# An adaptive layer norm block with a long convolution and a gated feed-forward: the inverse of an older step shares a PSUM bank with the spectrum of h, tables are built by half blocks, and loads change places

## The chip, the cores and the metric

The kernel runs on one core of a Trainium2 chip. Its engines are PE (TensorE: matmuls and transposes), DVE (VectorE), ACT (ScalarE), POOL (GpSimd) and SP (SyncE), which here issues all DMAs from one queue, in order. The metric is the device time in microseconds (us); lower is better. Before the change it is 1203.32 us, the median of three runs (1203.11 to 1203.95).

## The reference

One block of 2048 positions by 640 channels (D). A state space model gives each channel a kernel K as long as the sequence, and y is the causal convolution of h with K, written with Fourier transforms of twice the length. A gated feed-forward network of width 1728 follows. Cut to what matters:

```python
mod = (_silu(c) @ w_mod).reshape(c.shape[0], 6, 1, -1)
sa, ca, ga, sb, cb, gb = (mod[:, i] for i in range(6))
h = _layernorm(x) * (1 + ca) + sa
# _A_ref on h: 128 complex exponentials for each channel, summed
P = jnp.exp((A * dt[:, None])[:, :, None] * pos[None, None, :])
K = 2.0 * jnp.einsum("dn,dnl->dl", C, P).real
y = irfft(rfft(h, 2 * L) * rfft(K, 2 * L))[..., :L] + h * D_skip
x = x + ga * y
h = _layernorm(x) * (1 + cb) + sb
x = x + gb * ((_silu(h @ w1) * (h @ w3)) @ w2)
```

## The kernel before, in words

The channels are cut into five blocks of 128 (NB = 5). The work has these parts, which overlap.

- **h.** `h_stats` and `h_unit` normalise x (DVE, lines 257 and 260) and do the first stage of the transform of h as matmuls (line 267). The result goes to DRAM as h1.
- **Generation of K**, block by block (`gen_steps`). For each block, `param_part`, `param_exp` and `param_turn` make phases and decays, `param_exp` with eleven exponentials on ACT (line 340) into a tile E that has one buffer. `tables` builds small tables of powers by doubling: eight DVE instructions (lines 442 to 446) and twelve on POOL (line 449), for a block of 128 channels in one of two sets of tables. Then eight chunks of 16 channels each (`gen_chunk`) combine the tables: four POOL instructions (lines 480 and 486), three on ACT (sine, absolute value, cosine; lines 488 to 494), five on DVE (lines 498 to 502), and 32 small matmuls into kps (line 510; the profile counts 64 records). The next block's exponentials come with chunk 1, and its tables with chunks 2 to 6.
- **First stage of the transform of K** (`k_steps`): eight matmuls pk a block, copied to ko by ACT (line 575) and stored to DRAM as k1 (line 580). The last block does it in wide tiles (line 577).
- **The frequency stage** (`freq_steps`), also by block: 16 steps. A step has the spectrum of h (fh, line 602, evicted to fs by ACT, line 604), the spectrum of K (four matmuls fk, line 608), their product on DVE (fp, line 610), and, for the step two before (AH = 2), the first stage of the inverse (fz, two matmuls, line 619, evicted to zt, line 620). ht and kt are loaded for two steps at once (line 593); zt holds two steps, has two buffers, and is stored to DRAM as zd (line 622). fh, fk and fz each take a PSUM bank from the same three buffers (tag "f").
- **The last stage of the inverse** needs the factors wd, loads of zd (iz; for the last block of channels of the first rows izb; line 650), and x, to which its result is added. x lies in one tile x2 of 16 rows (j) per partition, and is loaded by `load_x2` (line 640). The first rows' inverse is done during the last frequency block (line 930).
- **The feed-forward** (`ffn`): second layer norm and transposes (`ln2`), then for four groups of 512 positions fourteen slices of the hidden width. `weights` loads a slice (w1 and w3 into wr, line 715 or 717; w2 into w2r, line 726 or 730) and splits it into a rounded part and a rest (lines 676 and 677, ACT and DVE). wr and w2r have two buffers each. The first slices are loaded before the feed-forward starts.

In the order of the program, block b's frequency stage lies beside the generation of block b + 1 and after. The order of the instructions on each engine is fixed when the program is built: a list scheduler takes the priorities that the kernel sets (`self.at`), and `order` adds an edge without a wait, which only says that one instruction is to stand behind another. On the chip each engine takes its instructions in that order, SP its DMA issues too.

Of the kernel before, what the change touches and what calls it, by code (L numbers as in the profile page):

```python
# [26 lines left out]
E4 = P // 4  # L27
EXPS = (1, 2, 4, 8, 16, 32)
# [69 lines left out]
class K:  # L98
# [318 lines left out]
    def table_sets(self):  # L417

        G = self.nc.gpsimd
        self.tabs = []  # L420
        for i in range(2):
            t = {nm: self.tbl.tile(sh, ty, name=f"{nm}{i}") for nm, sh, ty in (
                ("p1", [P, P, 2, 8], I32), ("p2", [P, P, 2, 4], I32),
                ("e1", [P, P, 2, 8], F32), ("e2", [P, P, 3, 4], F32))}
            G.memset(t["p2"][:, :, :, 0], 0)
            G.memset(t["e1"][:, :, :, 0], 1.0)
            G.memset(t["e2"][:, :, 2, 0], 1.0)
            self.tabs.append(t)
        self.step = self.tbl.tile([P, 4, 2, P], I32, name="step")

    def tables(self, b, part, parts, r=slice(0, P)):

        nc = self.nc
        V, G = nc.vector, nc.gpsimd
        t = self.tabs[b % 2]
        p1, p2, e1, e2 = (t[k] for k in ("p1", "p2", "e1", "e2"))
        E, st = self.E, self.step
        todo = []

        def steps():  # L440
            for a in range(2):
                V.tensor_scalar(p1[:, :, a, 0], self.pB[:, b, a], 0, None, op0=ALU.logical_shift_left)
            for k in range(1, 5):
                V.tensor_scalar(st[:, k - 1], self.pS[:, b], k, None, op0=ALU.logical_shift_left)
            for x, src in ((e2[:, :, 0, 0], self.mag[:, b]), (e2[:, :, 1, 0], E[:, 10])):
                V.tensor_copy(x, src)

        def double(tab, a, w, src, op):
            G.tensor_tensor(tab[:, r, a, w:2 * w], tab[:, r, a, 0:w], bc(src, len(src.shape), w), op=op)

        if r.start == 0:
            todo.append(steps)
        both = slice(0, 2)
        for tab, w, k in ((p2, 1, 3), (p2, 2, 4), (p1, 1, 0), (p1, 2, 1), (p1, 4, 2)):
            todo.append(lambda tab=tab, w=w, k=k: double(tab, both, w, (st[:, k - 1] if k else self.pS[:, b])[:, :, r].rearrange("p a t -> p t a"), ALU.add))
# [7 lines left out]
        return p1, p2, e1, e2  # L463


    def gen_chunk(self, d0, tabs, off, kps):
# [3 lines left out]
        p1, p2, e1, e2 = tabs  # L470
# [43 lines left out]
    def gen_steps(self, pc, ps):  # L514
# [7 lines left out]
        def chunk(c):  # L522
# [5 lines left out]
            self.gen_chunk(d0, self.cur, c * self.CD, st["kps"][:, (c % 2) * 256:(c % 2) * 256 + 256])  # L528
# [14 lines left out]
            if c == nch - 1:  # L543
                self.cur = self.nxt
# [41 lines left out]
    def freq_a(self, pc, fq, fpool, ps, bufs):  # L586
# [7 lines left out]
        return ht, kt, tl("zt")  # L594

    def freq_b(self, pc, fq, i, fpool, ps, bufs, held):

        nc = self.nc
        ht, kt, zt = held
        f = slice(2 * i, 2 * i + 2)  # L600
        ph = ps.tile([P, 512], F32, name=f"fh{pc}_{fq}{i}", tag="f", bufs=self.fb)[:, :2 * P].rearrange("p (f d) -> p f d", f=2)
        nc.tensor.matmul(ph, self.wh, ht[:, f, :], start=True, stop=True)  # L602
        hs = fpool.tile([P, 2, P], F32, name=f"fs{pc}_{fq}{i}", tag="fs", bufs=bufs["fs"])
        nc.scalar.activation(hs, ph, AF.Copy)
        pk = ps.tile([P, 2, 2, P], F32, name=f"fk{pc}_{fq}{i}", tag="f", bufs=self.fb)
        for g in range(2):
            for r in range(2):
                nc.tensor.matmul(pk[:, r, g], self.wb[:, 4 * fq + 2 * i + g, r, :], kt[:, 2 * i + g, :], start=True, stop=True)  # L608
        pp = fpool.tile([P, 2, 2, P], F32, name=f"fp{pc}_{fq}{i}", tag="fp", bufs=bufs["fp"])
        nc.vector.tensor_mul(pp, pk, bc(hs, 1, 2))  # L610
        return zt, pp

    def freq_c(self, pc, fq, i, ps, held):
        nc = self.nc
        o, n = pc * P, P
        zt, pp = held
        pz = ps.tile([P, 512], F32, name=f"fz{pc}_{fq}{i}", tag="f", bufs=self.fb)[:, :2 * P].rearrange("p (f d) -> p f d", f=2)
        for r in range(2):
            nc.tensor.matmul(pz, self.wz[:, r, :], pp[:, r], start=(r == 0), stop=(r == 1))  # L619
        nc.scalar.activation(zt[:, 2 * i:2 * i + 2], pz, AF.Copy)  # L620
        if i == 1:
            self.zlast = nc.sync.dma_start(self.zd[4 * fq:4 * fq + 4, :, :, o:o + n].rearrange("f r t d -> (r t) f d"), zt)

    def freq_steps(self, pc, fpool, ps, bufs, ahead=1):
        ha, hb = {}, {}

        def step(i):
            if i % 2 == 0 and i < 16:
                ha[i // 2] = self.freq_a(pc, i // 2, fpool, ps, bufs)
            if i < 16:  # L630
                hb[i] = self.freq_b(pc, i // 2, i % 2, fpool, ps, bufs, ha[i // 2])
            if i >= ahead:
                k = i - ahead
                self.freq_c(pc, k // 2, k % 2, ps, hb.pop(k))

        return [lambda i=i: step(i) for i in range(16 + ahead)]

    def load_x2(self, u, n, after):
        for q in range(4):
            self.order(self.nc.sync.dma_start(self.x2[q * 32:(q + 1) * 32, 2 * u:2 * (u + n)], self.xv[q, :, 2 * u:2 * (u + n), :]), after)  # L640
# [12 lines left out]
    def inverse(self, j0, nj, z, ps, tag, bufs, d0, d1, behind=None):  # L653
        nc = self.nc
        w = d1 - d0
        for j in range(nj):
            for o, n in ((0, w),) if w <= 512 else ((0, 320), (320, 320)):
# [7 lines left out]
                x2 = self.x2[:, j0 + j, d0 + o:d0 + o + n]  # L665
# [13 lines left out]
    def ln2(self, b, pool, ps, stats=None, tag="gu"):  # L679

        nc = self.nc
        xs = self.x2[:, b * 4:b * 4 + 4, :]
# [23 lines left out]
    def weights(self, b, m, wp):  # L706
# [3 lines left out]
        n = 2 if two else 1  # L710
        raw = wp.tile([P, 2, KT, P], F32, name=f"wr{b}_{m}", tag="wr", bufs=2)
        f0 = m * P
        for i, src in enumerate((self.w1, self.w3)):
            if two:
                nc.sync.dma_start(raw[:, i], src[:, f0:f0 + P].rearrange("(k p) f -> p k f", p=P))
            else:
                nc.sync.dma_start(raw[:, 0, :, i * 64:(i + 1) * 64], src[:, f0:].rearrange("(k p) f -> p k f", p=P))
# [7 lines left out]
        if two:  # L725
            nc.sync.dma_start(w2r, self.w2[m * P:(m + 1) * P, :])
            self.split(w2h, w2l, w2r, nc.vector)
        else:
            for i in range(2):
                nc.sync.dma_start(w2r[i * 64:(i + 1) * 64], self.w2[1664:1728, :])  # L730
# [75 lines left out]
    def output(self, b, acc, pool, ps):  # L806

        nc = self.nc
        for k in range(KT):
# [5 lines left out]
            xs = self.x2[:, b * 4:b * 4 + 4, k * P:(k + 1) * P]  # L815
            nc.vector.tensor_add(xs, pt.rearrange("p (j d) -> p j d", j=4), xs)
        for q in range(4):
            nc.sync.dma_start(self.ov[q, :, b * 4:b * 4 + 4, :], self.x2[q * 32:(q + 1) * 32, b * 4:b * 4 + 4, :])

    def run(self):  # L820
# [20 lines left out]
        e = open_("early", "right")  # L841
        self.gp = open_("gp")
# [16 lines left out]
        for r in (slice(0, 32), slice(32, P)):  # L859
            self.cur = self.tables(0, 0, 1, r)  # L860
# [26 lines left out]
        bufs = dict(ht=3, kt=3, fs=2, zt=2, fp=AH + 2)  # L887
        last = NB - 1
        stp = st0
        for pc in range(1, last + 1):  # L890
# [8 lines left out]
            for i, st in enumerate(self.freq_steps(pc - 1, fpool, psg, bufs, AH)):  # L899
# [8 lines left out]
        self.x2 = xp.tile([P, NJ, D], F32, name="x2")  # L908
        self.wd = ip.tile([P, NJ, 2, 64], F32, name="wd")
# [6 lines left out]
        for st in self.freq_steps(last, fpool, psg, bufs, AH):  # L916
# [8 lines left out]
        for u in range(2):  # L925
# [6 lines left out]
            x2 = self.x2[:, 2 * u:2 * u + 2, :cut]  # L932
            nc.vector.tensor_add(x2, py, x2)
            for j in (2 * u, 2 * u + 1):
                self.ln_part(stats[0], self.x2, j, 0, KT - 1)
# [9 lines left out]
        z = self.inverse_load("izb", ip, "izb", 1, 0, 4, cut, D)  # L945
        self.inverse(0, 4, z, ps, "gu", 3, cut, D)
# [13 lines left out]
        close("ps", "po", "ffn", "wp", "ip", "xp")  # L960
# [30 lines left out]
```

## Time and profile before

| | |
|---|---|
| median of the runs | 1203.32 us |
| the profiled execution | 1206.13 us |
| its span, first to last instruction | 1204.4 us |
| PE / DVE / ACT / POOL busy | 1018.2 / 690.0 / 503.2 / 307.6 us |
| mean granted TensorE clock | 0.921 |
| moved by DMA | 157.61 MB, mean 131 GB/s |

The page shows the span in 40 slices of 30 us, each digit a busy share in tenths. A row of the chain of waits has a start, a length, and what was busy or awaited. A row of an engine's timeline has start, length, engine, line, what is written from what, and how many were merged. In a row of groups the two last numbers are the busy sum and the mean of one. SPq rows are DMA issues on SP. Matmuls of fp32 operands appear as two records each.

### The profile page before, as it was taken

Reading aid. Unit: us, or ns where it says so; the run is one execution under the profiler, and the core shown is the slowest. Engines: PE = TensorE matmul, PEld = TensorE weight load, DVE = VectorE, ACT = ScalarE, POOL = GpSimd, SP = SyncE. Lnnn points to the kernel's source line nnn. Section 1 sums busy time; section 2 is a strip of 40 time slices with the busy share of each in tenths; the row PEclk is TensorE's granted clock in tenths of the full one; section 3 lists DMA queues with packets and bytes.
Section 4 is the critical chain, followed back from the end, with each engine's and each line's share of the span. In section 5 each row is a group of like instructions: output and inputs, shape, how many; then the busy total and the mean of one; then the engine's idle time right before and its main releaser. Section 6 shows DMA issues by size and latency. Waiting matters only on the chain.

```text
span 1204.4 us, 17748 instructions
## 1 busy us (share of the span) xinstructions
PE 1018.2 (85%) x6737; PEld 763.4 (63%) x6737; DVE 690.0 (57%) x1184; ACT 503.2 (42%) x838; POOL 307.6 (26%) x269
## 2 busy tenths in 40 slices
PE   2347774975977995797599999999999999999996
PEld 0124432753764764766377788888888888888885
DVE  7999969578477741231564384543735445354332
ACT  3344775566376753222242243433424333343221
POOL 5677577677488710000000000000000000000000
PEclk9577985998897998989699999999999999999999
DMA  8955875424426359878656333533335332353311
GB/s 247 248 161 139 229 251 125 114 79 80 123 75 128 107 136 232 236 174 200 164 133 159 92 88 88 140 95 83 98 88 133 108 98 72 83 144 97 99 45 44
DMA packets 205502, 157.61 MB, mean 131 GB/s; under 512 B 55912, under 2 KB 187880, under 8 KB 204008
## 3 DMA queue, kind: packets, MB, share of 16 engines
q1 hardware_dynamic: 205416, 156.48, 49.6%
q8 instruction: 53, 0.87, 0.3%
q14 instruction: 33, 0.27, 0.1%
HBM read 119.74 MB, written 36.70 MB: 130 GB/s over the span
## 4 chain that ended last, share of the span: by engine, by line
PE 66%; DVE 13%; DMA 10%; ACT 4%; issue 3%; POOL 2%; SPq 2%; DVEq 0%; ACTq 0%
PE gu L763 11%; PE gu L765 10%; PE gu L764 10%; PE fk L608 5%; PE acc L798 5%; PE acc L800 5%; PE acc L799 5%; PE fz L619 4%; DMA zd<-zt 3%; PE fh L602 3%; PE kps L510 3%; DVE xs L257 2%; DMA kt<-k 1%; DMA xt<-in_x 1%; DVE xs L260 1%
## 5 line engine op out<-in xcount | busy, mean ns | idle before, releaser
L763 PE MATMUL gu<-xh,wh 128*128 128x512 f32 x540 | 213.7, 396 | 0.0
L764 PE MATMUL gu<-xl,wh 128*128 128x512 f32 x540 | 213.4, 395 | 0.0
L765 PE MATMUL gu<-xh,wl 128*128 128x512 f32 x540 | 213.2, 395 | 0.0
L676 ACT ACTIVATE wh<-wr 128x640 fp32r<-128x640 f32 x108 | 74.2, 732 | 145.3 <-PE gu L764 136.4
L610 DVE TENSOR_TENSOR fp<-fk,fs 128x512 f32<-128x512 f32 x80 | 54.9, 687 | 127.6 <-PE fk L608 108.6
L732 POOL MEMSET w2l<- 64x640 f32 x4 | 2.5, 628 | 456.2 <-PE acc L799 456.2
L763 PEld LDWEIGHTS gu<-xh,wh 128*128 128x128 f32 x540 | 101.4, 188 | 25.7 <-issue 1.0
L765 PEld LDWEIGHTS gu<-xh,wl 128*128 128x128 f32 x540 | 101.3, 188 | 25.1 <-issue 0.5
L764 PEld LDWEIGHTS gu<-xl,wh 128*128 128x128 f32 x540 | 101.4, 188 | 24.8 <-issue 0.5
L510 PEld LDWEIGHTS kps<-yy,xx 128*32 128x32 f32 x2560 | 58.7, 121 | 86.9 <-issue 57.1
L608 PE MATMUL fk<-kt,wb 128*128 128x128 f32 x640 | 97.0, 299 | 19.4 <-DMA kt<-k 15.0
L510 PE MATMUL kps<-yy,xx 128*32 128x64 f32 x2560 | 77.9, 244 | 38.7 <-DVE xx L502 33.5
L608 PEld LDWEIGHTS fk<-kt,wb 128*128 128x128 f32 x640 | 89.5, 209 | 29.7 <-DMA kt<-k 11.1
L798 PE MATMUL acc<-ah,w2h 128*128 128x512 f32 x260 | 104.6, 402 | 0.0
L799 PE MATMUL acc<-ah,w2l 128*128 128x512 f32 x260 | 102.7, 395 | 0.0
L800 PE MATMUL acc<-al,w2h 128*128 128x512 f32 x260 | 98.4, 395 | 0.0
L486 POOL TENSOR_TENSOR yy<-e,e 128x512 f32<-128x512 f32 x80 | 88.4, 1129 | 32.1 <-PE kps L510 31.6
L619 PE MATMUL fz<-fp,wz 128*128 128x256 f32 x320 | 87.6, 399 | 9.5 <-ACT zt L620 9.5
L677 DVE TENSOR_TENSOR wl<-wr,wh 128x640 fp32r<-128x640 f32 x108 | 84.7, 818 | 17.1 <-ACT wh L676 17.1
L778 DVE SCALAR_TENSOR_TENSOR a<-th,gu 128x512 f32<-128x512 f32 x52 | 35.7, 686 | 99.8 <-ACT th L777 99.6
L779 DVE TENSOR_TENSOR a<-a,gu 128x512 f32<-128x512 f32 x52 | 35.8, 688 | 96.2 <-PE gu L765 96.2
L777 ACT ACTIVATE th<-gu 128x512 f32<-128x512 f32 x52 | 31.1, 598 | 127.5 <-PE gu L765 127.5
(191 smaller groups left out, 1743.8 us busy)
## 6 DMA issues: line engine op xcount, KB each, us to landing
wr<-in_w SPq DMA_DIRECT2D x104, 320.0 KB
w2r<-in_w SPq DMA_DIRECT2D x52, 320.0 KB
h<-ho SPq DMA_DIRECT2D x32, 320.0 KB
k<-ko SPq DMA_DIRECT2D x40, 256.0 KB
ht<-h SPq DMA_DIRECT2D x40, 256.0 KB
kt<-k SPq DMA_DIRECT2D x40, 256.0 KB
zd<-zt SPq DMA_DIRECT2D x40, 256.0 KB
wm<-in_w_mod SPq DMA_DIRECT2D x10, 960.0 KB
```

The lines of the kernel that those rows point to most:

```text
L486: G.tensor_tensor(out.rearrange("p d (k i) -> p d k i", k=4), bc(t1, 2, 4), bc(t2, 3, 8), op=ALU.mult)
L510: nc.tensor.matmul(kps[q * 32:(q + 1) * 32, e * 64:(e + 1) * 64], xx[:, r, i, :], yy[:, r, i, :, :].rearrange("p a b -> p (a b)"), start=( ...
L608: nc.tensor.matmul(pk[:, r, g], self.wb[:, 4 * fq + 2 * i + g, r, :], kt[:, 2 * i + g, :], start=True, stop=True)
L619: nc.tensor.matmul(pz, self.wz[:, r, :], pp[:, r], start=(r == 0), stop=(r == 1))
L676: self.nc.scalar.activation(H, v, AF.Copy)
L677: eng.tensor_tensor(Lo, v, H.bitcast(F32), op=ALU.subtract)
L763: nc.tensor.matmul(pg, wh[:, i, k, :], xh[:, k, :], start=(k == 0), stop=False)
L764: nc.tensor.matmul(pg, wh[:, i, k, :], xl[:, k, :], start=False, stop=False)
L765: nc.tensor.matmul(pg, wl[:, i, k, :], xh[:, k, :], start=False, stop=(k == KT - 1))
L798: nc.tensor.matmul(acc[k], w2h[:, sl], ah, start=(m == 0), stop=False)
L799: nc.tensor.matmul(acc[k], w2l[:, sl], ah, start=False, stop=False)
L800: nc.tensor.matmul(acc[k], w2h[:, sl], al, start=False, stop=(m == 12))
```

## The change

1. In the frequency stage one PSUM bank takes the spectrum of h of step i and the first inverse stage of step i - 2, and one ACT instruction evicts both into a tile hz of three buffers. The product reads one half of hz, and the store of z the other half. A store now covers one step (two of the frequencies), so there are 80 stores in place of 40. The tiles fs and zt go. A block has 18 evictions: 14 of 512 elements a partition and four of 256.
2. The tables are built for half blocks of 64 channels. One set serves chunks 0 to 3 and the other chunks 4 to 7. The second half is built with chunks 1 to 3 of its own block, the first half of the next block with chunks 5 to 7, and the next block's exponentials come with chunk 3. The tables take half the memory.
3. In that memory x for the first four rows (x2[0]) and wd get places that are free from the start; x2 becomes four tiles. Both are loaded when the program reaches pc == 3, behind the last kt load of the frequency block just issued.
4. The other three tiles of x are loaded behind the izb loads. The weights that are loaded ahead are ordered behind the last kt load of the frequency stage.

```diff
@@ tables
-                ("p1", [P, P, 2, 8], I32), ("p2", [P, P, 2, 4], I32),
-                ("e1", [P, P, 2, 8], F32), ("e2", [P, P, 3, 4], F32))}
+                ("p1", [P, HB2, 2, 8], I32), ("p2", [P, HB2, 2, 4], I32),
+                ("e1", [P, HB2, 2, 8], F32), ("e2", [P, HB2, 3, 4], F32))}
-    def tables(self, b, part, parts, r=slice(0, P)):
+    def tables(self, b, h, part, parts, r=slice(0, HB2)):
-        t = self.tabs[b % 2]
+        t = self.tabs[h]
+        hs = slice(h * HB2, h * HB2 + HB2)
+        E, st, pS = self.E[:, :, hs], self.step, self.pS[:, b, :, hs]
@@ gen_steps
-            self.gen_chunk(d0, self.cur, c * self.CD, ...)
+            self.gen_chunk(d0, self.tabs[c // 4], c % 4 * self.CD, ...)
+            if 1 <= c < 4:
+                self.tables(pc, 1, c - 1, 3)
-                if c == 1:
+                if c == 3:
                     self.param_exp(self.pp, ps, pc + 1)
                     self.param_turn(self.pp, ps, pc + 1)
-                if 2 <= c < 7:
-                    self.nxt = self.tables(pc + 1, c - 2, 5)
+                if c > 4:
+                    self.tables(pc + 1, 0, c - 5, 3)
@@ freq_steps
+            pa = ps.tile([P, 2, 2, P], F32, name=f"fa{pc}_{i}", tag="f", bufs=self.fb)
+            hz = fpool.tile([P, 2, 2, P], F32, name=f"hz{pc}_{i}", tag="hz", bufs=bufs["hz"])
             if i < 16:
+                nc.tensor.matmul(pa[:, 0], self.wh, ht[:, g0:g0 + 2, :], start=True, stop=True)
+            if i >= lag:
+                pp = prod.pop(i - lag)
+                for r in range(2):
+                    nc.tensor.matmul(pa[:, 1], self.wz[:, r, :], pp[:, r], start=(r == 0), stop=(r == 1))
+            sl = slice(0 if i < 16 else 1, 2 if i >= lag else 1)
+            nc.scalar.activation(hz[:, sl], pa[:, sl], AF.Copy)
+            if i >= lag:
+                f = 2 * (i - lag)
+                self.zlast = nc.sync.dma_start(self.zd[f:f + 2, :, :, pc * P:pc * P + P].rearrange("f r t d -> (r t) f d"), hz[:, 1])
...
+                nc.vector.tensor_mul(prod[i], pk, bc(hz[:, 0], 1, 2))
@@ weights
+        dma = lambda out, src: self.order(nc.sync.dma_start(out, src), after)
@@ run
+        first = open_("first")
+        self.x2 = [first.tile([P, 4, D], F32, name="x20")]
+        self.wd = first.tile([P, NJ, 2, 64], F32, name="wd")
-        bufs = dict(ht=3, kt=3, fs=2, zt=2, fp=AH + 2)
+        bufs = dict(ht=3, kt=3, hz=3, fp=4)
+            if pc == 3:
+                self.load_x2(0, self.load)
+                self.order(nc.sync.dma_start(self.wd, self.t_wd), self.load)
-        self.load_x2(0, 2, mid_load)
-        self.order(nc.sync.dma_start(self.wd, self.t_wd), mid_load)
-        self.load_x2(2, 6, self.load)
+        wload = self.load
         for m in range(WA):
-            self.ahead[0, m] = self.weights(0, self.ORDER[m], wp)
+            self.ahead[0, m] = self.weights(0, self.ORDER[m], wp, wload)
         z = self.inverse_load("izb", ip, "izb", 1, 0, 4, cut, D)
+        for b in range(1, 4):
+            self.load_x2(b, self.zload)
```

More of the change, by code (lines that the diff above doesn't have):

```diff
@@ L27 @@
 E4 = P // 4
+HB2 = P // 2
 EXPS = (1, 2, 4, 8, 16, 32)
@@ L469, in gen_chunk @@
         V, A, G = nc.vector, nc.scalar, nc.gpsimd
-        p1, p2, e1, e2 = tabs
+        p1, p2, e1, e2 = (tabs[k] for k in ("p1", "p2", "e1", "e2"))
         w = self.gw
@@ L527, in chunk @@
                 st["kps"] = ps.tile([P, 512], F32, name=f"kps{pc}_{c}", tag="kg", bufs=1)
-            self.gen_chunk(d0, self.cur, c * self.CD, st["kps"][:, (c % 2) * 256:(c % 2) * 256 + 256])
+            self.gen_chunk(d0, self.tabs[c // 4], c % 4 * self.CD, st["kps"][:, (c % 2) * 256:(c % 2) * 256 + 256])
             if c % 2 == 1:
@@ L593, in freq_a, with freq_steps @@
             self.load = nc.sync.dma_start(t, src[4 * fq:4 * fq + 4, :, :, o:o + n].rearrange("f r s d -> (r s) f d"))
-        return ht, kt, tl("zt")
-    def freq_b(self, pc, fq, i, fpool, ps, bufs, held):
+        return ht, kt
+    def freq_steps(self, pc, fpool, ps, bufs):
         nc = self.nc
[L599 to L622, printed above, removed]
@@ L624, in freq_steps @@
-    def freq_steps(self, pc, fpool, ps, bufs, ahead=1):
-        ha, hb = {}, {}
+        held, prod = {}, {}
+        lag = 2
         def step(i):
             if i % 2 == 0 and i < 16:
-                ha[i // 2] = self.freq_a(pc, i // 2, fpool, ps, bufs)
+                held[i // 2] = self.freq_a(pc, i // 2, fpool, ps, bufs)
+            pa = ps.tile([P, 2, 2, P], F32, name=f"fa{pc}_{i}", tag="f", bufs=self.fb)
+            hz = fpool.tile([P, 2, 2, P], F32, name=f"hz{pc}_{i}", tag="hz", bufs=bufs["hz"])
@@ L630, in step @@
             if i < 16:
[L631 to L638, printed above, removed]
+                ht, kt = held[i // 2]
+                g0 = i % 2 * 2
+                nc.tensor.matmul(pa[:, 0], self.wh, ht[:, g0:g0 + 2, :], start=True, stop=True)
@@ new lines, in step @@
+            if i < 16:
+                pk = ps.tile([P, 2, 2, P], F32, name=f"fk{pc}_{i}", tag="f", bufs=self.fb)
+                for g in range(2):
+                    for r in range(2):
+                        nc.tensor.matmul(pk[:, r, g], self.wb[:, 2 * i + g, r, :], kt[:, g0 + g, :], start=True, stop=True)
+                prod[i] = fpool.tile([P, 2, 2, P], F32, name=f"fp{pc}_{i}", tag="fp", bufs=bufs["fp"])
+                nc.vector.tensor_mul(prod[i], pk, bc(hz[:, 0], 1, 2))
+        return [lambda i=i: step(i) for i in range(16 + lag)]
@@ L639, in load_x2 @@
+    def load_x2(self, b, after):
         for q in range(4):
-            self.order(self.nc.sync.dma_start(self.x2[q * 32:(q + 1) * 32, 2 * u:2 * (u + n)], self.xv[q, :, 2 * u:2 * (u + n), :]), after)
+            self.order(self.nc.sync.dma_start(self.x2[b][q * 32:(q + 1) * 32], self.xv[q, :, 4 * b:4 * b + 4, :]), after)
     def inverse_load(self, name, pool, tag, bufs, j0, nj, d0, d1):
@@ L681, in ln2 @@
         nc = self.nc
-        xs = self.x2[:, b * 4:b * 4 + 4, :]
+        xs = self.x2[b]
         st, mv = stats or self.ln_begin(pool, f"n{b}")
@@ L704, in ln2, with weights @@
         return xh, xl
-    def weights(self, b, m, wp):
+    def weights(self, b, m, wp, after=None):
         nc = self.nc
@@ L858, in run @@
         self.load_c(e)
-        for r in (slice(0, 32), slice(32, P)):
-            self.cur = self.tables(0, 0, 1, r)
+        for r in (slice(0, 16), slice(16, HB2)):
+            self.tables(0, 0, 0, 1, r)
         self.at(-800)
@@ L898, in run @@
                 st()
-            for i, st in enumerate(self.freq_steps(pc - 1, fpool, psg, bufs, AH)):
+            for i, st in enumerate(self.freq_steps(pc - 1, fpool, psg, bufs)):
                 self.at(v0 + 50 + 50 * i)
@@ L907, in run @@
         xp, ip, wp = open_("xp"), open_("ip"), open_("wp")
-        self.x2 = xp.tile([P, NJ, D], F32, name="x2")
-        self.wd = ip.tile([P, NJ, 2, 64], F32, name="wd")
+        self.x2 += [xp.tile([P, 4, D], F32, name=f"x2{b}") for b in range(1, 4)]
         self.ahead, self.turn = {}, 0
@@ L915, in run @@
         self.at(1000 * last + 1000)
-        for st in self.freq_steps(last, fpool, psg, bufs, AH):
+        for st in self.freq_steps(last, fpool, psg, bufs):
             st()
         self.at(1000 * last + 2000)
-        self.load_x2(0, 2, mid_load)
-        self.order(nc.sync.dma_start(self.wd, self.t_wd), mid_load)
-        self.load_x2(2, 6, self.load)
         stats = self.ln_begin(ip, "n0")
@@ L959, in run @@
         self.ffn(nxt, wp, pool, ps, po, mid)
-        close("ps", "po", "ffn", "wp", "ip", "xp")
+        close("ps", "po", "ffn", "wp", "ip", "xp", "first")
 def emit(tc, io):
```

32 lines of the change are left out of this document (14 added, 18 removed).

## The prediction, on record before the changed kernel ran

> **What bounds the kernel now.** I read the slices of the page first, then stretches of 30 us, then the chain of waits and SP's rows in the stretch that stood out.
>
> ```profile
> PE   2347774975977995797599999999999999999996
> ...
> DMA  8955875424426359878656333533335332353311
> ```
>
> From slice 21 on (600 us) PE is full to the end: the feed-forward part takes as long as its matmuls, and the change touches none of them. What can move lies before. In stretches (PE, PEld, DVE, ACT, POOL busy; granted clock, DMA share, GB/s):
>
> ```profile
> 420.00:450.00 30.00, 30.00 (x325) 19.98 (x325) 12.99 (x20) 15.85 (x28) 5.88 (x6) 1.00 0.50 126
> 450.00:480.00 30.00, 17.13 (x80) 11.78 (x79) 5.87 (x8) 10.29 (x18) 0.00 (x0) 0.83 0.98 229
> ...
> 540.00:570.00 30.00, 22.42 (x130) 19.77 (x128) 7.62 (x17) 6.42 (x17) 0.00 (x0) 0.94 0.88 201
> 570.00:600.00 30.00, 16.05 (x79) 10.96 (x79) 14.80 (x47) 8.28 (x12) 2.56 (x2) 0.66 0.63 149
> ```
>
> Generation ends at 441. The last two frequency blocks then stand alone, PE waits, and the DMA engines are full. The chain of waits names what for (start, length, what):
>
> ```profile
> 489.87 0.43 PE fh L602 x2
> 490.30 0.89 PE fk L608 x8
> 491.19 0.87 PE fz L619 x4
> ...
> 494.88 15.87 DMA zd<-zt x2
> ...
> 551.35 19.15 DMA zd<-zt
> ...
> 573.47 2.28 DMA zd<-zt
> ```
>
> A step needs 0.43 + 0.89 + 0.87 = 2.19 us of PE. A store of z alone lands in 2.28 us; twice it took 16 to 19, and an eviction (zt has two buffers) waited for it. SP's rows show what was queued ahead:
>
> ```profile
> 546.10 0.96 SPq L640 DMA_DIRECT2D x<-in_x  x2
> 547.15 0.38 SPq L622 DMA_DIRECT2D zd<-zt  x1
> 547.58 1.50 SPq L640 DMA_DIRECT2D x<-in_x  x2
> 551.35 22.49 SPq L622 DMA_DIRECT2D zd<-zt  x4
> 575.94 2.56 SPq L650 DMA_DIRECT2D izb<-zd  x4
> 578.54 26.18 SPq L650 DMA_DIRECT2D iz<-zd  x16
> ```
>
> The four x loads hold 3.93 MB. The same at 493.8 to 496.5, with 1.31 MB of x and 1.05 MB of wd.
>
> **The change, part by part.** Three marks: f0 (first fk of block 0, 211.2), f3 (first fk of block 3, 470.1), t0 (first izb issue, 575.9). After t0 come 20 us of layer norm, then the feed-forward.
>
> *Shared eviction.* 80 fs of 385 ns and 80 zt of 381 ns make 61.3 us; now 70 of 512 elements and 20 of 256. A PSUM copy of 512 is the ko row of L575, 594 ns: 70 x 0.594 + 20 x 0.383 = 49.2. So 12 us of ACT go, 2.4 per block. In the last two blocks ACT is busy 6 to 10 of 30 us, so this is worth 0. The added wait: the eviction now stands behind the two fz matmuls (0.87), and the product behind it. PE's fk (0.89) runs meanwhile, so a step stays at 2.19: 0. A step takes two of the three PSUM banks where it took all three, which can only help. Bounds: a gain of 2.4 per block; a loss where the eviction stands behind the sine, abs and cosine of a chunk (1.04 + 1.06 + 1.12 = 3.2 us) in each mixed block, some 10 in all.
>
> *Stores of z.* 80 of 128 KB for 40 of 256 KB. SP spends 0.36 us on one that waits for nothing: 8 x 0.36 = 2.9 per block, beside waits. What counts is the slot: hz has three, each held until its store has landed, and now the spectrum stands in it too. Three steps are 6.6 us, a store 2.28: 0, unless loads are queued ahead. The Trainium skill (DMA: Bandwidth & Descriptors, Rules for kernel authors) speaks against this: many small transfers are to be merged; its section Anatomy of one DMA puts the fixed part of a DMA at about 2.0 us, with which the 2.28 of the lone store agrees. By that figure eight more stores would be an estimated 16 us in the last block, if they were waited for in turn.
>
> *Tables by halves.* The 85 us of L449 are 17 per block. Pairs of rows of double size (569/909, 909/1425, 1425/2365, 1611/2386) say that a half costs 0.60 to 0.68 of the whole: about +4.5 us of POOL per block. POOL stands idle 55.7 us for DVE's xx and 31.6 for PE's kps: 0, at most 18 over four blocks if that cover is gone. DVE's table steps (2 x 1.16 + 4 x 0.52 + 0.38 + 0.33 = 5.1 per block) become 16 of half size, +1 to +5.
>
> The order of the instructions shows what this moves. DVE has 174 us of rows ahead of its last scaling of x before and 178 after, 219 and 227 ahead of the first product. DVE is full from 60 to 150 and busy 48 of the next 60, so f0 comes about 6 us later (0 to 8): 217. From there generation falls back. Chunks done in the running block where blocks 0 to 3 of the frequency stage start: 6, 7, 8, 8 before; 7, 4.8, 4, 5.8 after.
>
> *f0 to f3* is 258.9 us. After, it holds 22.8 chunks in place of 26. A chunk alone is 1.96 us of PE (64 records at 290.7) and 5.4 of POOL (2.02 + 2 x 1.13 + 1.14). PE bounds the mixed blocks, so 2: -6. The holes between blocks (first pk to first fk) are 30, 22 and 31 us; the third has seven weight loads in front of the k stores and no chunks left. At the mean of the other two, with 3.6 chunks in it: -5, and -3 since PE has work there. The transposes for the next exponentials stood within blocks 1 and 2, where PE then idled 5.6 and 5.2; now they stand at the end of the hole, where the kt load is awaited anyway: -6 of 11. The x and wd loads in block 1 are 2.36 MB, 10 us at 230 GB/s against three steps of 3.3: +3. Together 242 (230 to 250), f3 = 459, 11 us earlier.
>
> *f3 to t0* is 105.8 us now: 32 steps are 70, the first inverse 6.6, the rest waits. After: steps 70, inverse 6.6, 2.2 chunks 4.3, the last pk 7 (they lay in the hole before) make 88; switching 3; the wait for the last k store and kt, and for z stores behind the iz loads, 7 (0 to 12). Then the weights. They now follow the last kt, four tiles and 3.5 MB between the last eight stores, and ACT's order has their roundings between the evictions of steps 10 to 14, each waiting for its landing. In the third hole the same loads took SP from 441.0 to 462.7, 21.7 us; 4 more for the last steps and the landing make 25.7, against 17.5 of PE for eight steps: +8 (0 to 23). Sum 106: no change. The x loads go, the weights take their place.
>
> *After t0.* 3.93 MB of x stand between izb and the iz loads of units 2 and 3. Now those two (2.6 MB) have landed by 592, t0 + 16. With x ahead, at 225 to 250 GB/s, 16 to 17.5 us later: t0 + 33. PE reaches them at t0 + 19 and has some 6 us of matmuls of its own between: +7 (3 to 11).
>
> Sum: 6 - 17 + 0 + 7 = **-4 us**. To that comes what I can't see and set at -2: the clock, 0.83 and 0.66 in stretches with holes that are now filled. -6 on the profiled execution (1206.1, span 1204.4), which is 2.8 above the median of the runs; on the median 1203.3 - 6 = **1197**.
>
> **Rivals.**
> 1. *The holes close* (18%). Nothing bounds generation that PE doesn't; PE is busy only 214 of 270 us from 180 to 450. f0 to f3 at 230, the weights hidden by half: -12 - 4 further, **1181**. For it: the third hole has no x or weights. Against: the first hole is 30 us without either.
> 2. *The feed-forward's start eats the gain* (15%): x ahead of iz costs 11 in place of 7, **1202**, within 0.2% (what a measurement of this kernel can tell from no change, 2.4 us).
> 3. *Slower* (29%): the last eight steps are paced by stores in turn with the weights. Place: after the last kt. Price: 21.7 of weights and eight stores of 2.28, 18.2, in series: 40 in place of 25.7, +14, **1211**. It decides once those steps take over 34 us. For it: the slot of the store now holds the spectrum too, and 551.35 shows the like. Against: SP issues the loads over 16 us, not in 4. The Trainium skill's rule above would make it worse.
>
> **Numbers.** Forecast 38%, all faster by over 0.2%; with rival 1 faster 56%, same 15%, slower 29%. The outer rivals are known to 3 us or so; a range from 1178 to 1213 leaves out about a tenth on either side.
>
> **What would show it.** Right: no z store of over 10 us between f3 and the last kt; f3 near 459; the k stores right behind the transforms in the third hole; a gap of PE after the first five gu matmuls, ended by iz; evictions of steps 11 to 14 waiting for wr. Wrong: f3 at 470 or later (tables or evictions pace generation), POOL idle for nothing but E, or t0 later than 576.

## The result and the profile after

Slower by 0.3%: the median is 1206.95 us over 20 runs (1202.09 to 1209.56), beside 1203.06 over 20 runs of the kernel before on the same chip (1199.54 to 1206.51); ratio 1.0029, 95% interval [1.0017, 1.0041]. The profiled execution has a span of 1205.2 us (1207.0 with what lies around it), clock 0.914. The profile of before was one of its longer executions, so the two profiles differ by only 0.8 us; the other 3 us of the difference between the medians cannot be read from them.

By the marks of the prediction (us):

| stretch | before | forecast | after |
|---|---|---|---|
| start to f0, first fk of block 0 | 211.2 | 217 | 211.2 |
| f0 to f3, first fk of block 3 | 258.9 | 242 | 241.7 |
| f3 to t0, first izb issue | 105.8 | 106 | 110.9 |
| t0 to the end of the span | 628.5 | 635.5 | 641.5 |

The first izb issue comes 12.2 us earlier, about as forecast, and the feed-forward's start then loses 13.0. The slices (PE and DMA), and stretches of 30 us with the columns of before:

```profile
PE   2357673895996989895699999999999999999996
...
DMA  9957648335365454778956333533335332353311
```

```profile
420.00:450.00 30.00, 24.98 (x370) 16.03 (x370) 19.44 (x28) 22.66 (x30) 22.30 (x19) 0.92 0.56 113
450.00:480.00 30.00, 28.96 (x285) 23.86 (x286) 12.63 (x19) 9.96 (x14) 5.65 (x5) 0.85 0.45 126
540.00:570.00 30.00, 19.07 (x108) 15.86 (x107) 8.79 (x13) 7.67 (x14) 0.00 (x0) 0.85 0.79 214
570.00:600.00 30.00, 17.94 (x61) 10.96 (x60) 13.06 (x39) 6.85 (x8) 2.55 (x2) 0.64 1.00 221
```

The hole with full DMA engines at 450 to 480 is gone (PE 17.1 to 29.0, DMA share 0.98 to 0.45). The last row has a DMA share of 1.00 (0.63 before), and PE, which could be in the feed-forward 12 us sooner, works 17.9 us of 30 there (16.1 before) at a clock of 0.64. The chain of waits names what it waits for:

```profile
543.86 6.71 DMA wr<-in_w
...
556.16 5.25 DMA zd<-hz
...
568.90 9.51 DMA x<-in_x
578.42 11.76 DMA iz<-zd
...
590.31 4.50 PE iy L655 x8
```

No z store is waited for 16 to 19 us any more. After 568 the x loads and, behind them, the z loads carry the chain for 21 us. The timelines of SP and of PE:

```profile
563.75 2.60 SPq L644 DMA_DIRECT2D izb<-zd  x4
566.39 9.34 SPq L634 DMA_DIRECT2D x<-in_x  x12
577.07 31.36 SPq L644 DMA_DIRECT2D iz<-zd  x15
```

```profile
582.38 0.79 PE L758 MATMUL gu<-xh,wh 128*128 128x512 f32 x1 [0.49 <-ACT xh L695]
...
584.25 0.63 PE L759 MATMUL gu<-xl,wh 128*128 128x512 f32 x1
590.31 4.50 PE L655 MATMUL iy<-iz,wd 128*64 128x320 f32 x8 [5.43 <-DMA iz<-zd]
...
597.52 2.37 PE L655 MATMUL iy<-iz,wd 128*64 128x320 f32 x10
```

and PE's before:

```profile
593.17 2.91 PE L661 MATMUL iy<-iz,wd 128*64 128x320 f32 x20
596.01 0.50 PE L763 MATMUL gu<-xh,wh 128*128 128x512 f32 x1
```

PE is at its first gu matmul, the first of the feed-forward, 13.6 us earlier than before (582.4 against 596.0), does five of them, and stands behind an iy that waits for its z. PE takes its instructions in order, so the gu matmuls behind it wait too. Before, twenty iy ran ahead of the first gu and none waited.

### The profile page after: what moved, and what is told of

Read it like the earlier page. It is cut to its first block, busy times and chain, and to the rows that moved or that the text cites. A ratio compares the mean times of both kernels' runs of the same rounds, so it can differ in the third digit from the quotient of the medians.

```text
span 1205.2 us, 17828 instructions
## 1 busy us (share of the span) xinstructions
PE 1029.8 (85%) x6737; PEld 777.4 (65%) x6737; DVE 696.6 (58%) x1224; ACT 495.2 (41%) x768; POOL 316.6 (26%) x329
## 4 chain that ended last, share of the span: by engine, by line
PE 70%; DVE 14%; DMA 7%; ACT 3%; issue 2%; SPq 2%; POOL 1%; DVEq 0%; ACTq 0%
PE gu L760 11%; PE gu L758 10%; PE gu L759 10%; PE fk L626 6%; PE fa L616 5%; PE acc L793 5%; PE acc L795 5%; PE acc L794 5%; PE fa L612 3%; PE kps L511 3%; PE iy L655 2%; DMA k<-ko 1%; DMA xt<-in_x 1%; DVE xs L258 1%; DVE step L446 1%
## 5 line engine op out<-in xcount | busy, mean ns | idle before, releaser
L511 PE MATMUL kps<-yy,xx 128*32 128x64 f32 x2560 | 83.5, 247 | 53.3 <-DVE xx L503 28.3
L511 PEld LDWEIGHTS kps<-yy,xx 128*32 128x32 f32 x2560 | 61.6, 123 | 101.4 <-issue 53.9
L760 PEld LDWEIGHTS gu<-xh,wl 128*128 128x128 f32 x540 | 101.5, 188 | 26.4 <-issue 2.0
L628 DVE TENSOR_TENSOR fp<-fk,hz 128x512 f32<-128x512 f32 x80 | 54.8, 686 | 98.1 <-PE fk L626 97.8
L626 PE MATMUL fk<-kt,wb 128*128 128x128 f32 x640 | 99.8, 305 | 13.1 <-DMA kt<-k 12.3
L618 ACT ACTIVATE hz<-fa 128x512 f32<-128x512 f32 (+1 forms) x90 | 49.2, 547 | 126.5 <-PE fa L616 105.6
L795 PE MATMUL acc<-al,w2h 128*128 128x512 f32 x260 | 98.1, 395 | 0.0
```

The lines of the kernel that those rows point to most:

```text
L511: nc.tensor.matmul(kps[q * 32:(q + 1) * 32, e * 64:(e + 1) * 64], xx[:, r, i, :], yy[:, r, i, :, :].rearrange("p a b -> p (a b)"), start=( ...
L626: nc.tensor.matmul(pk[:, r, g], self.wb[:, 2 * i + g, r, :], kt[:, g0 + g, :], start=True, stop=True)
L760: nc.tensor.matmul(pg, wl[:, i, k, :], xh[:, k, :], start=False, stop=(k == KT - 1))
L795: nc.tensor.matmul(acc[k], w2h[:, sl], al, start=False, stop=(m == 12))
```

## The experiments

Fourteen kernels ran, each timed against the kernel before. The marks are those of each run's profile; the ratio is to the kernel before, with its 95% interval.

| kernel | f0 to f3 | f3 to t0 | t0 to end | median | ratio |
|---|---|---|---|---|---|
| changed kernel | 241.7 | 110.9 | 641.5 | 1206.95 | 1.0029 [1.0017, 1.0041] |
| iz_first | 243.4 | 110.0 | 630.3 | 1194.08 | 0.9926 [0.9907, 0.9946] |
| no_x | 243.4 | 109.5 | 630.5 | 1195.85 | 0.9939 [0.9914, 0.9963] |
| weights_early | 241.8 | 111.5 | 628.2 | 1193.61 | 0.9935 [0.9912, 0.9958] |
| old_loads | 242.8 | 129.7 | 629.5 | 1212.68 | 1.0083 [1.0064, 1.0103] |
| only_evict | 236.5 | 130.0 | 630.4 | 1209.48 | 1.0060 [1.0038, 1.0081] |
| only_tables | 260.5 | 100.1 | 629.8 | 1202.70 | 1.0004 [0.9989, 1.0019] |
| sep_evict | 255.6 | 86.4 | 629.6 | 1181.11 | 0.9829 [0.9807, 0.9852] |
| e_two | 224.9 | 108.7 | 629.5 | 1175.94 | 0.9789 [0.9766, 0.9813] |
| both | 238.5 | 91.6 | 628.7 | 1174.38 | 0.9761 [0.9739, 0.9783] |
| order_back | 239.2 | 85.8 | 630.1 | 1166.39 | 0.9698 [0.9674, 0.9722] |
| order_e | 238.8 | 86.2 | 628.9 | 1178.81 | 0.9779 [0.9741, 0.9817] |
| after_order | 241.9 | 87.1 | 641.8 | 1180.24 | 0.9807 [0.9782, 0.9832] |
| sep_order | 249.7 | 87.1 | 629.3 | 1179.69 | 0.9794 [0.9769, 0.9818] |
| before_order | 258.9 | 100.0 | 629.8 | 1201.26 | 0.9986 [0.9971, 1.0001] |

The column of t0 to the end is worth a look first: there every kernel takes 628 to 631 us, except the two with x ahead of the z loads (641.5 and 641.8).

### Is it x ahead of the z loads?

**iz_first.** The theory was that the order within SP's queue alone stalls the feed-forward; rivals were the roundings of weights, now behind the first tanh, and DVE's need of x.

```diff
         z = self.inverse_load("izb", ip, "izb", 1, 0, 4, cut, D)
+        zs = [self.inverse_load(f"iz{u}", ip, "iz", 2, 2 * u, 2, 0, D) for u in range(2, IU)]
         for b in range(1, 4):
             self.load_x2(b, self.zload)
...
         for u in range(2, IU):
-            self.inverse_unit(u, ip, po, None, 1, self.behind)
+            self.inverse(2 * u, 2, zs[u - 2], po, None, 1, 0, D, self.behind)
```

> The changed kernel with one edit: the z loads of units 2 and 3 are issued right behind izb, and the twelve x loads of blocks 1 to 3 behind them. Theory (the 3.93 MB of x ahead of those z loads is what stalls the start of the feed-forward): nothing moves up to the first izb issue at about 564; the z loads land by about 580, before PE has done its five first gu matmuls (585 in the changed kernel), the 5.4 us wait and the slow first iy group go, and the stretch from izb to the end shrinks from 641 to about 630: about 1195 to 1198, ratio to before 0.993 to 0.996. Rival (the 13 us lie in the roundings of weights 1 and 2, which now stand behind the first tanh, or in the later wr of tile 3): PE gets its iy early but idles later in the first gu tiles, 1204 to 1207, ratio 1.001 to 1.004. Second rival (the x loads are only put off: DVE's adds of units 2 and 3 need x of block 1, and the five PSUM banks of iy fill): half of it stays, 1200 to 1202.

1194.08 us: one microsecond under the theory's 1195 to 1198, and 1.0% (12 us) under the changed kernel. Its timelines of SP and PE:

```profile
561.70 2.60 SPq L644 DMA_DIRECT2D izb<-zd  x4
564.33 5.09 SPq L644 DMA_DIRECT2D iz<-zd  x8
569.46 15.03 SPq L634 DMA_DIRECT2D x<-in_x  x12
```

```profile
579.77 4.31 PE L655 MATMUL iy<-iz,wd 128*64 128x320 f32 x20
584.01 0.50 PE L758 MATMUL gu<-xh,wh 128*128 128x512 f32 x1
```

The same twelve x loads take SP longer (15.0 us) and nobody waits: the twenty iy run ahead of the first gu without a bracket behind them, as before the change.

**no_x** removes the loads instead: `nc.gpsimd.memset(self.x2[b], 0.5)` in place of `self.load_x2(b, self.zload)`, in the changed kernel. It leaves x out of the sum in three of the four blocks of rows.

> The changed kernel without the loads of x of blocks 1 to 3: those tiles are set to a constant on GpSimd, so the residual of three of the four blocks is left out of the sum. It prices these 3.93 MB. Theory (they cost only by standing ahead of the z loads): like iz_first, from izb to the end 628 to 630, 1192 to 1196, ratio 0.991 to 0.995. Rival (behind the z loads they still cost something, DVE's adds wait for x of block 1): 1186 to 1191. Rival (the 13 us were something else, the coincidence of iz_first being the weights' later wait): 1200 or more.

1195.85 us, the same as iz_first within the intervals. Behind the z loads 3.93 MB cost nothing that can be measured; ahead of them, 12 us. The rivals of both runs fall.

### Which part of the change does what?

**old_loads**, **only_evict**, **only_tables** take the change apart. old_loads is the changed kernel with every load where before has it. The other two are the kernel before with one part of the diff each.

> The changed kernel with every load where before has it: x of block 0 and wd behind the kt of the mixed blocks, x of blocks 1 to 3 behind the last kt, weights free to go early. Shared eviction and half tables stay. Theory (tables and eviction gain some 8 us up to the fourth block by themselves; moving the weights out of the third hole gave the other 9, moving x cost 13 after izb): f3 at 459 to 463, izb at about 565 to 572, from izb to the end 628 to 629, so 1195 to 1202, ratio 0.993 to 0.999. Rival (the slots of the shared tile stand behind the x loads in the last block and eat what the tables gain): f3 as above, but izb at 576 or later, 1204 to 1210. Second rival (the gain up to f3 was the moved loads alone): f3 at 468 or later, 1202 to 1206.

> The kernel before with the shared PSUM bank and eviction (and its 128 KB stores of z) alone. Prediction's step: 0, bounds -10 to +10. If it holds: f0 211, f3 470 within 2, izb 576 within 4, 1200 to 1206, ratio 0.998 to 1.002. Rival (smaller stores and a third shared slot pay in turn behind the x loads): izb 579 to 586, ratio 1.003 to 1.008. Rival (ACT's 12 us are worth something in the mixed blocks): f3 465 or earlier, ratio under 0.997.

> The kernel before with the tables by half blocks alone. Prediction's steps: f0 +6, then -6 fewer chunks, -3 for the holes with PE work in them, -6 exponentials; the third hole keeps its weights; behind f3 the last chunks and last transforms come on top, +11. Seen in the changed kernel: f0 did not slip. If tables alone make the earlier f3: f0 211, f3 458 to 463, ratio 0.994 to 1.000. Rival (they pay only with the shared eviction, ACT being the engine that chunks and steps share in the mixed blocks): f3 465 to 472, ratio 1.000 to 1.006.

My theory for old_loads failed: 1212.68, as its first rival had it and 3 us beyond, with izb at 584.2. only_evict is slower by 0.6%, with the ratio of its first rival and an f3 (447.4) far below that of its second; only_tables is the same as before, as its rival had it, with f3 at 471.9. What surprised me is the order of the instructions. Chunks done where blocks 0 to 3 of the frequency stage start:

```text
before         14.0  23.0  32.0  40.0
only_tables    15.0  23.8  32.9  40.0
only_evict     14.0  20.0  27.6  37.8
after          15.0  20.8  28.0  37.8
```

The prediction had put the falling back of generation down to the tables. It comes with the shared eviction: the scheduler, given the new steps, places more of them ahead of the chunks. (Why it does was not traced.) So the transforms of the fifth block land behind the start of the fourth block's steps. In SP's timeline of only_evict, with the loads in their old places:

```profile
477.32 1.84 SPq L633 DMA_DIRECT2D x<-in_x  x4
...
492.50 4.87 SPq L580 DMA_DIRECT2D k<-ko  x4
...
510.08 2.63 SPq L580 DMA_DIRECT2D k<-ko  x2
...
552.12 23.52 SPq L620 DMA_DIRECT2D zd<-hz  x7
```

x, wd and weights stand ahead of the fifth block's k stores, which take from 492 to 513, and the last seven z stores stand behind x, 23.5 us for them (22.5 for four in before). f3 comes earlier, and f3 to t0 takes 130 where before takes 106.

**sep_evict** and **weights_early** undo one part each in iz_first: the steps with their own banks and evictions, and `wload` left out.

> The run with the z loads first (iz_first, 0.993 of before), with one part of the change undone: spectrum and inverse have a bank and an eviction each again, z is stored 256 KB at a time. Tables by halves and all loads stay as in iz_first. The instruction order then has 40 chunks done before the fourth block starts (as before), not 37.8. Theory (the shared eviction gains nothing: alone it cost 7 us; what it did was to move chunks behind the fourth block's start): f3 at 460 to 466 (the third hole without weights), izb at 556 to 562, 1186 to 1194, ratio 0.986 to 0.993. Rival (its cost came only from stores queued with the x loads, and with those gone it pays): izb 565 or later, 1196 to 1202, ratio 0.995 to 1.000.

> iz_first with one part of the loads undone: the weights of tiles 0, 13, 1 and 2 are not ordered behind the last kt and go as soon as their buffers are open. The prediction priced their move at -5 in the third hole and +8 among the last eight stores. Theory (they stand ahead of the fifth block's k stores, whose transforms now lie behind the fourth block's start, as in the kernel with only the shared eviction, where that hole took 30 us): the hole from the first pk of block 4 to its first fk grows from 23.7 to about 32, the last eight steps gain some of it back; izb 564 to 570, 1196 to 1203, ratio 0.995 to 1.001. Rival (the weights cost the same wherever they go): 1192 to 1196, ratio 0.991 to 0.995.

sep_evict: 1181.11, 1.0% better than iz_first and 5 us better than the theory's 1186 to 1194; the hole behind f3 goes (86.4 in place of 110.0), and f0 to f3 grows by 12. weights_early: 1193.61, the rival: the weights cost the same in either place. That move is worth nothing. What the new places of x and wd are worth, with the z loads first, shows in two pairs of runs: 1.7% (21 us) from only_tables to sep_evict, and 1.6% (19 us) from old_loads to iz_first, though the weights move as well in both. Of the parts of the change, only these places gained by themselves.

### Is it the eviction or the order?

**order_back** changes one number of iz_first.

```diff
-                self.at(v0 + 50 + 50 * i)
+                self.at(v0 + 800 + 50 * i)
```

> iz_first with one number changed: the priorities of the frequency steps begin at 800 in place of 50, so that the instruction order has 24.0, 32.6 and 40 chunks done where blocks 1, 2 and 3 of the frequency stage start (23.8, 32.9, 40 in sep_evict; 20.8, 28.0, 37.8 in iz_first) and the transforms of the fifth block lie ahead of the fourth block's steps again. The shared eviction, its slots and its 128 KB stores stay. Theory (what the shared eviction costs is this order: the fifth block's k makes its way out and back, 24 us from its first transform to its first product, with no chunk and few steps beside it): that hole goes as in sep_evict, izb at 546 to 552, 1180 to 1186, ratio 0.982 to 0.987. Rival (the eviction behind two more matmuls, the three slots and the small stores cost by themselves): izb at 556 or later, 1189 to 1196, ratio 0.989 to 0.995.

1166.39 us, better than either line of the expectation: 2.3% (27 us) under iz_first, 3.0% under before, and 15 us under sep_evict. The theory holds for the order; neither line had room for a shared eviction that gains. PE's timeline of iz_first, around the fifth block's way out to DRAM and back:

```profile
485.86 3.60 PE L574 MATMUL pk<-ks,wk 128*128 128x512 f32 x8
...
503.46 0.59 PE L612 MATMUL fa<-ht,wh 128*128 128x256 f32 x2
509.53 2.05 PE L626 MATMUL fk<-kt,wb 128*128 128x128 f32 x8 [5.47 <-DMA kt<-k]
```

and of order_back:

```profile
439.33 5.63 PE L574 MATMUL pk<-ks,wk 128*128 128x512 f32 x8 [5.61 <-ACT ko L578]
446.27 1.13 PE L626 MATMUL fk<-kt,wb 128*128 128x128 f32 x8 [1.31 <-DMA kt<-k]
```

In iz_first the trip from the first pk (485.9) to the first fk of that block (509.5) takes 23.7 us, with 4 steps' work left to fill it. In order_back the fifth block's transforms (evicted by L578) stand in the hole of the fourth block, ahead of f3 at 446.3, and f3 to t0 takes 85.8 in place of 110.0. f0 to f3 does not pay for it: 239.2 against 243.4, with all 40 chunks and these transforms in it. There the chunks' matmuls (kps) keep PE busy for 39.2 us with 1600 records, in iz_first for 51.5 with 1460.

**sep_order**, **after_order** and **before_order** followed, to close what was open: sep_evict with 600 in place of 50 (order 15.0, 24.0, 33.0, 40.0, order_back's but for 0.4 of a chunk), the changed kernel itself with 800, and the kernel before with 600.

> sep_evict (own evictions, z loads first, 0.983 of before) with its priorities moved to 600, which gives 15.0, 24.0, 33.0 and 40 chunks before the four blocks, where order_back, with the shared eviction, has 15.0, 24.0, 32.6 and 40. Now only the eviction and its stores differ. Theory (with an equal order the shared eviction pays, in the mixed blocks, where ScalarE also has the chunks): 1178 to 1184, ratio 0.980 to 0.985, f0 to f3 about 255 where order_back has 239. Rival (order_back is ahead because its order is better, whatever the eviction): 1164 to 1171, ratio 0.968 to 0.974.

> The changed kernel as it is, x ahead of the z loads too, with the one number of order_back (priorities of the frequency steps from 800). If the two losses add up (12 for x ahead of the z loads, 28 for the order): 1176 to 1182, ratio 0.978 to 0.983. If the order's gain needs the z loads first: 1190 or more.

> The control: the kernel before with nothing but its priorities moved to 600 (15.0, 24.0, 33.5 and 40 chunks before the blocks, where it has 14, 23, 32 and 40). If the number only mends what the shared eviction did to the order: 1200 to 1206, ratio 0.997 to 1.003. If later steps are better for any version of this kernel: 1195 or less, ratio under 0.994.

All three fell on the theory, by their times. sep_order 1179.69 against order_back 1166.39: at nearly equal chunk counts the shared eviction is worth 1.0% (0.9794 to 0.9698), 10.5 us of it between f0 and f3. PE's waits hardly shrink there: their sum is 46.7 us in sep_order and 45.7 in order_back. What shrinks is its busy time, 205.9 us in sep_order and 195.5 in order_back, and of it above all that of the chunks' matmuls, 48.4 and 39.2 for the same 1600 records. Two rows, of order_back and of sep_order, show the difference:

```profile
223.37 1.17 PE L511 MATMUL kps<-yy,xx 128*32 128x64 f32 x64
```

```profile
227.99 0.43 PE L511 MATMUL kps<-yy,xx 128*32 128x64 f32 x12
```

In order_back the 25 chunks of this stretch stand in 52 pieces between the steps' matmuls, ten of them whole chunks of 64 records; in sep_order in 82, four of them whole. Equal chunk counts are thus not yet an equal order, and how much of the 1.0% is the eviction itself and how much the way steps and chunks alternate stays open. after_order 1180.24: the two losses of the changed kernel add up, 27 us for the order and 13 for x. before_order 1201.26, not told from before: the number mends what the shared eviction did, and is no gain of its own.

### The late exponentials

**e_two** gives E two buffers in iz_first, `self.tables` takes its block's, and `param_exp` goes back from `c == 3` to `c == 1`.

> iz_first with two buffers for the exponentials, so that they can be made in the second chunk again instead of the fourth. Theory of the prediction's step (the late exponentials are hidden in holes where kt is awaited anyway): no change, 1192 to 1196, ratio 0.991 to 0.995. Rival (the table work that waits for the late exponentials stalls the next chunks, DVE's wait for E is 24.9 us in two places and PE waits 10.1 us for xx in the first hole): the first hole shrinks by 4 to 8 us, f1 287 or earlier, 1186 to 1191, ratio 0.986 to 0.991.

1175.94: better than the rival, 18 us under iz_first (16.5 by the ratios), and in the profiles all of it between f0 and f3 (224.9 against 243.4). The waits from 200 to 450 us (total, times, longest), of iz_first:

```profile
DVE e L448 <- ACT E L341: 24.9, 2, 14.8
...
PE kps L511 <- DVE xx L503: 18.5, 4, 10.1
```

and of e_two:

```profile
PE kps L513 <- DVE xx L505: 17.1, 6, 4.4
DVE e L450 <- ACT E L343: 15.0, 2, 11.1
```

The table work waits for the exponentials, and the chunk behind it holds PE for 10.1 us in one piece in the first hole; with two buffers the longest is 4.4. DVE's wait for E falls by 10 us. Between f0 and f3 PE's idle time falls from 41.8 to 27.2 us, and its busy time from 202.6 to 197.5, at a clock of 0.91 in place of 0.88. The edit also moves chunks a little (14.5, 20.0, 27.6 and 37.7 done where the blocks start), so it is priced as a whole.

**both** joins this to sep_evict, **order_e** to order_back.

> Tables by halves and the change's loads, with the two edits that gained: z loads first, own evictions for spectrum and inverse (as in sep_evict, 0.983) and the exponentials in the second chunk, from two buffers (as in e_two, 0.979). If the two gains (13 and 18 us against iz_first) are apart: 1160 to 1166, ratio 0.965 to 0.970. If they are partly the same (both shorten the time to the end of the chunks): 1167 to 1174, ratio 0.970 to 0.977. If only one counts: 1175 to 1181.

> The shared eviction kept, with the order put back (as in order_back) and the exponentials in the second chunk (as in e_two). It stands beside the run with own evictions and early exponentials. If the shared eviction itself costs nothing: within 3 us of that run. If it costs by its stores and slots: 6 to 12 us above it. If its 12 us less of ScalarE pay once the order is right: 3 us or more below it.

both: 1174.38, by its ratio within its second case, and not told apart from e_two alone: the gains overlap almost wholly. order_e: 1178.81, 4.4 us above both, between the lines of its expectation; but its runs lie between 1168.55 and 1183.26, and its profile, of the shortest of them, is 4.6 us longer than that of order_back. It shows that early exponentials do not add to order_back; the intervals say that they lose, but the 4.6 us between the profiles lie ahead of f0 (212.8 against 207.0), and why the runs spread is open. order_back is the best version that ran.

## Why the prediction was wrong

It said 1197 and faster. The sum on the profiles was -6; measured, +0.8, and +3.9 between the medians. Two steps failed above all: the price of x ahead of the z loads, and the one that gave the shared eviction's steps their old place beside the chunks.

- **After t0, +7 (3 to 11): the term that decided, measured 13.** The mechanism was right, down to the gap behind the first five gu matmuls. The step that failed is "PE reaches them at t0 + 19 and has some 6 us of matmuls of its own between: +7", which priced a wait and nothing else. PE was there at t0 + 18.6, and its own work in front of the first iy was five matmuls, 2.5 us and not 6; what stands behind a waiting instruction is no cover. That iy needed only the first of the z loads, which had landed by t0 + 26.4; the t0 + 33 of the prediction is for all of them. These two errors met in a wait of 5.4.

  The other 7.6 us were put at nothing. This iy and the 17 after it took 6.9 us (about 2.6 at the pace of before's twenty in 2.91: 4.3 more): no wait is recorded between them, but most start one by one, the first eight 0.53 us apart, where before's start two at a time, 0.27 apart. The matmuls around the gap ran at half clock (about 1.7 more), and PE came to this place 1.4 us later after t0 than before (17.2). That makes 12.8 of the 13. Why the iy ran one by one was not traced. Rival 2 was this very case with 11 (its sum gives 1201, where it says 1202), and had 15%.
- **f0 to f3, -17: measured -17.2, by luck, for its parts were wrong.** "Fewer chunks" was there, but from the shared eviction's order, not from the tables (only_tables: 260.5, only_evict: 236.5), and it saved PE nothing: the chunks' matmuls keep it busy for 51.5 us where before has 50.3, with 3.2 chunks less. The 1.96 us of "a chunk alone" is that of a chunk behind a wait of 5.23 us; the whole chunk in order_back takes 1.17. "Exponentials -6" had the wrong sign: e_two shows that they cost 16 to 18 in this order. What did go is the fifth block's transforms (pk 33.7 to 25.4 us) and PE's wait for their copies (9.4 us). Errors of opposite sign met in a right sum.
- **Shared eviction, 0: wrong twice.** The durations were right (90 evictions, 49.2 us busy, as worked out) and the small stores cost little: in the changed kernel evictions wait for them five times, 13.8 us in all. But its order costs 27 us, and at a good order the kernel with it is about 12 faster (the 2.4 per block that the prediction named as a bound would be 10 in the four mixed blocks; but the gain shows in PE's chunks, not in its waits). The step that failed is "a step stays at 2.19: 0", which priced the step and not where the scheduler then puts it. The order after the change was known when I predicted; I read the chunk counts from it and put them down to the wrong part.
- **f3 to t0, 106: measured 110.9.** The move of the fifth block's transforms was in the sum as 7 us of work and a wait of 7 (0 to 12). PE was busy for 98.1 us of it where the forecast's work is 88, and the +8 for the weights did not come. The hole of the fifth block is 23.7 us long (iz_first), and 86 would have been to be had. A forecast against the old time alone did not ask for that.
- **Weights, -5 and +8:** weights_early says 0 for both together. (SP's rows of before show ten weight loads ahead of the fourth block's last k store, not seven.)
- **f0, +6:** measured 0. Over the profiles of all these kernels f0 lies between 205 and 213, so a term of this size is not told. That it failed to come was luck too: with it the sum would have been 6 us further off.
- **The clock, -2:** 0.921 became 0.914. The hole at 450 to 480 went, but the one at 570 to 600 stayed, and f0 to f3 ran at 0.88 where before ran at 0.91.
- **Rival 3** (stores in turn with the weights) did not come: the longest of those five waits is 3.7 us, where before had 16 to 19. Stores behind x did come back, in only_evict and old_loads, where x kept its old place. The Trainium skill (DMA: Bandwidth & Descriptors, Rules for kernel authors) says that many small transfers are to be merged, and that under 64 KB one pays mostly overhead; the stores here are larger. order_back has 80 of 128 KB and is faster than sep_order with 40 of 256 KB, but the evictions differ as well, so no run here prices the stores alone. The 2.0 us by which the prediction sized them is given in the Trainium skill (DMA: Bandwidth & Descriptors, Anatomy of one DMA) for DMAs issued from GpSimd, while here SP issues; in the changed kernel a 128 KB store landed after 1.9 us (median of 80).
- **The signs** of being right were seen (f3 at 452.9, the k stores right behind their transforms, no z store above 5.25 us in the chain, the gap ended by iz, 5.0 us of ACT's waits for wr), and none of being wrong. None of them asked how long PE needs behind that gap, or what stands between f3 and t0.

## What to carry to other kernels

A load that is wanted late must not stand in the queue ahead of one that is wanted soon: the same bytes cost 12 us in front and nothing behind. Where a scheduler sets the order, price an edit by the new order before its own instructions, and find out which edit moved what; here one number in the priorities was worth 27 us, where the whole change lost 4. A right total is no proof of its parts.

## What the runs showed of the hardware

In these traces a wait of PE costs more than its length. After 5.47 us without work the eight fk matmuls of iz_first took 2.05 us, after 1.31 us in order_back 1.13. In the changed kernel the five gu matmuls ahead of the gap at 584.9, themselves behind shorter waits, took 0.63 to 0.79 us, the first gu behind it 0.74, and later ones 0.39; the first eight iy behind it start 0.53 us apart, later ones 0.27. The Trainium skill (TensorE: Matmul & The Clock Gate, Part 1: The HAM clock gate) says that the clock is either half or full, and half until PE has been busy for a while; the 0.53 and 0.27 agree. How long a while, these runs do not show.

Small matmuls in short pieces took longer each. In order_back a whole chunk of 64 kps records held PE for 1.11 us (223.37 until the next matmul at 224.48), in sep_order 12 records for 0.36 (227.99 until 228.35): 17 and 30 ns a record.
